# The channel MLP's second layer: 256 features per bank visit instead of 128

## The chip, the cores and the metric

The kernel runs on one core of a Trainium2 chip (trn2). The core has five engines that run side by side and wait for each other by semaphores: TensorE (PE in the profile; its weight loads are listed apart as PEld), VectorE (DVE), ScalarE (ACT), GpSimd (POOL) and SyncE (SP), which issues most of the DMAs from one queue, in order. The metric is the device time of one execution in microseconds (us); lower is better.

## The reference

Attention with a threshold, per batch row (8 of them) and head (8), over 576 tokens of 64 features, and then an MLP mixer on the row of 576 tokens by 512 features:

```python
scores = scale * np.matmul(q, k.transpose(0, 1, 3, 2))
thresh = np.max(scores, axis=-1, keepdims=True) - tau
scores = np.where(scores >= thresh, scores, -1000000000.0)
...
attn = attn / (np.sum(attn, axis=-1, keepdims=True) + 1e-09)
out = np.matmul(attn, v)
# heads side by side: x is (8, 576, 512)
h = np.maximum(x.transpose(0, 2, 1) @ w_tok1, 0.0) @ w_tok2
u = x + h.transpose(0, 2, 1)
h2 = np.maximum(u @ w_ch1, 0.0) @ w_ch2
return u + h2
```

`w_tok1` is 576 x 256, `w_tok2` 256 x 576, `w_ch1` 512 x 1536 and `w_ch2` 1536 x 512. All is float32. The last two lines are the channel MLP; its second layer is the product with `w_ch2`.

## The kernel before

The program is emitted by a planner (`Scheduler`). Each piece of work is an operation with an engine, an estimated cost, a rank and the operations it depends on. The planner keeps a clock for each engine, picks whatever can start first (at equal times the lower rank), and calls the function that emits its instructions. The order so found is each engine's program order on the chip; the estimates are used for nothing else.

Attention runs in 72 rounds, 9 to a batch row. A round is: scores on TensorE (S, L825), row maxima on VectorE (`mx`, L842), a bias on GpSimd (`bias`, L848), masks on ScalarE (L858), exponentials on ScalarE (L868), a scaling on GpSimd (L285), a blockwise transpose on VectorE (`T`, L315) and its completion by DMA (`eT<-T`, L327). Three units of such probabilities make one product with the values (V, L365 and L370). While attention of row b runs, the MLPs of the row before fill TensorE between the rounds: the token MLP (turns L435, first layer L454, second layer L472, added into `xT` by L483) and then, for a group of 256 tokens, the channel MLP. A round of rows 1 to 7 is held back until enough of that filling has been done (`self.done` against a plan), as long as there is other work for TensorE.

The channel MLP of a group is, for rows 1 to 6 (one group each; row 0 has two, which are done in another way, and what is put off is done after attention, by other code, from 903 us on):

- `turn_u` (L933, VectorE) transposes the group blockwise into the tile `us`, and `move_u` (SyncE, L940) completes it into `ut`. `us` is one buffer: it can be written only when the stores of the group before have read it.
- `ch1` (L948), 12 outputs of 4 products, each followed by a ReLU into `g` on ScalarE (L953) or VectorE (L956).
- `ch2` (L964), for each of 2 blocks of 128 tokens 4 outputs of 128 features, each the sum of 12 products; `leave` (L978, VectorE) adds the residual from `ut` and writes into `us`.
- `store` (L988, SyncE), one per block of tokens, when the block's outputs are in `us`.

Outputs of TensorE go to PSUM banks. While attention runs, two banks serve everything but the scores: values, token MLP and channel MLP. `banked` makes a pair of operations, the products, which take a free bank, and the eviction, which frees it; the products of an output are one piece and can't be interrupted. On VectorE, ScalarE and SyncE, too, an instruction that waits holds up all that is behind it in the order.

The spill of `xT` (L531) and the moves into `x_sb` (L406, L412) are other DMAs in SyncE's order. On the page, float32 products have two records each, so that an output of `ch2` shows as 24 records of L964.

Of the kernel before, what the change touches and what calls it, by code (L numbers as in the profile page):

```python
# [17 lines left out]
P = 128  # L18
# [3 lines left out]
def kernel(  # L22
# [38 lines left out]
    NCC = DM // P  # L61
    NJ = DCH // P
# [7 lines left out]
    work = ctx.enter_context(tc.tile_pool(name="work", bufs=2))  # L70
# [74 lines left out]
    wc2 = const.tile([P, NJ, DM], F32, name="wc2")  # L145
# [233 lines left out]
    class Step:  # L379


        def __init__(self, kind, cost, on, cost_out, work, leave, other=None):
            self.kind, self.cost, self.on, self.cost_out, self.work, self.leave = kind, cost, on, cost_out, work, leave
            self.other = other
# [167 lines left out]
    class Op:  # L552

        def __init__(self, eng, cost, fn, deps, after, rank, lag, row, index):
            self.eng, self.cost, self.fn, self.rank, self.lag, self.row, self.index = eng, cost, fn, rank, lag, row, index
            self.end, self.bank, self.frees, self.later, self.open, self.other = None, None, None, [], 0, None
            self.dmas, self.landed, self.shared = None, None, False
            self.deps = [d for d in deps if d is not None]
            for d in self.deps + [d for d in after if d is not None]:
                if d.end is None:  # L560
                    d.later.append(self)
                    self.open += 1
# [5 lines left out]
    class Scheduler:  # L568
# [22 lines left out]
        def banked(self, cost, work, on, cost_out, leave, deps=(), rank=5, row=None, rank_out=0, other=None):  # L591
            x = self.op("pe", cost, work, deps, rank, row=row)
            y = self.op(on, cost_out, leave, (x,), rank_out, row=row, other=other)
            x.bank = True
            y.frees = x
            return x, y

        def sure(self, x):
            t = max([d.landed + SPARE if d.landed else d.end + d.lag + SLACK * (d.eng != x.eng) for d in x.deps] + [0.0])
            if x.bank:  # L600
                t = max(t, min(b.free for b in self.banks if b.free is not None) + SLACK)
            return t
# [59 lines left out]
        def run(self, until):  # L662
            while not until():
                best = None
                for e in self.clock:
                    c = self.pick(e)
                    if c and (best is None or c[0][0] < best[0][0]):
                        best = c + (e,)
                if best is None:
                    assert all(x.end is not None for x in self.ops), [(x.eng, x.rank, x.index, x.open) for x in self.ops if x.end is None][:20]  # L670
                    return
                _, t, x, eng = best
                if eng == "pe" and t < WARM_UNTIL:
                    self.keep_warm(t)
                self.ready[x.eng].remove(x)
                if x.other:
                    self.ready[x.other[0]].remove(x)
                    if eng != x.eng:
                        x.eng, x.cost, x.fn = x.other
                if x.dmas:  # L680
                    x.end = self.transfer(t, *x.dmas)
                    x.landed = self.in_flight[-1]
                else:
                    x.end = t + x.cost
                self.clock[x.eng] = x.end
                if x.eng == "pe":
                    self.last_rank = x.rank
                if x.bank:
                    b = min((b for b in self.banks if b.free is not None), key=lambda b: b.free)
                    b.free = None  # L690
                    x.bank = b, b.pool.tile([P, MAIN], F32, tag=b.tag, name=f"bank_{x.index}")
                    x.fn(x.bank[1])
                    if x.row is not None:
                        self.done += x.cost
                elif x.frees:
                    b, tile_ = x.frees.bank
                    x.fn(tile_)
                    b.free = x.end + 0.15
                else:
                    x.fn()  # L700
                for y in x.later:
                    y.open -= 1
                    if not y.open:
                        self.enter(y)

    sched = Scheduler()
# [3 lines left out]
    def key_op(*key):  # L710
        return keyed.get(key)
# [165 lines left out]
    fills = {}  # L877
# [41 lines left out]
    def make_groups(b, halves):  # L919
        uT = xTs[b]  # L920
        reads = []
        for i in range(NOW[b]):
            s = {}
            n, nt = GR, GR // P

            def new_us(s=s, i=i):
                s["us"] = work.tile([P, nt, 4, NCC * 32], F32, tag="us", bufs=1, name=f"us_{b}_{i}")
# [27 lines left out]
            def relu_v(bank, j, s=s):  # L955
                nc.vector.tensor_scalar(out=s["g"][:, j, 0:n], in0=bank[:, 0:n], scalar1=0.0, scalar2=None, op0=ALU.max)  # L956

            def ch2(bank, t, c, s=s, i=i):
                to = bank[:, 0:P]
                t0 = GR * i + P * t  # L960
                if not b:
                    nc.tensor.matmul(to, lhsT=uT[:, c, t0 : t0 + P], rhs=ident, is_transpose=True, start=True, stop=False, skip_group_check=True)
                for j in range(NJ):
                    nc.tensor.matmul(  # L964
                        to,
                        lhsT=s["g"][:, j, P * t : P * t + P],
                        rhs=wc2[:, j, P * c : P * c + P],
                        start=(j == 0 and b > 0),
                        stop=(j == NJ - 1),
                        skip_group_check=True,  # L970
                    )

            def leave(bank, t, c, s=s):
                if not b and "us" not in s:
                    new_us(s)
                o = s["us"][:, t].rearrange("q a x -> q (a x)")[:, P * c : P * c + P]
                if b:
                    nc.vector.tensor_add(  # L978
                        out=o.rearrange("q (k d) -> q k d", k=4),
                        in0=bank[:, 0:P].rearrange("q (k d) -> q k d", k=4),  # L980
                        in1=s["ut"][:, t][:, :, 32 * c : 32 * c + 32],
                    )
                else:
                    nc.scalar.copy(out=o, in_=bank[:, 0:P])
# [12 lines left out]
            for j in range(NJ):  # L997
                x, y = sched.banked(
                    1.79,
                    lambda bank, j=j, f=ch1: f(bank, j),  # L1000
                    "act",
                    0.29,
                    lambda bank, j=j, f=relu: f(bank, j),
                    have + state["ch2"] + [key_op("pool", 7 + j)],
                    2,
                    b,
# [5 lines left out]
            seconds, stores, adds = [], [], []  # L1012
            for t in range(nt):
                outs = []
                for c in range(NCC):
                    x, y = sched.banked(
                        2.7 if b else 2.8,
                        lambda bank, t=t, c=c, f=ch2: f(bank, t, c),
                        "dve" if b else "act",
                        0.21,  # L1020
                        lambda bank, t=t, c=c, f=leave: f(bank, t, c),
                        relus + moved + (converted if not b else []) + (state["stores"] if not b else []),
                        2,
                        b,
                        1 if b else 0,
                    )
                    outs.append(y)
                    seconds.append(x)
                    if not b:
                        reads.append(x)  # L1030
                    fills[b] = fills.get(b, 0.0) + x.cost
                adds += outs
                stores.append(sched.op("sp", 0.35, lambda t=t, f=store: f(t), outs, 2, dmas=(1, 150, 0.35)))
            state["ch2"], state["stores"], state["adds"] = seconds, stores, adds
# [453 lines left out]
```

## Time and profile before

| | us |
|---|---|
| three runs | 1269.9, 1270.09, 1276.9 |
| median | 1270.09 |
| the profiled execution | 1273.39 |
| its span, first to last instruction | 1271.4 |
| mean granted TensorE clock | 0.991 |

| stage of the profiled execution | us | TensorE busy |
|---|---|---|
| 0 to 205: attention of rows 0 and part of 1, weights converted | 205.0 | 188.8 |
| 205 to 903: attention and the MLPs of the row before | 698.0 | |
| 903 to 1271.4: the token groups that were put off | 368.4 | 363.2 |

The profile is one execution on the chip. A row of the groups gives the line and engine, the operation, out<-in by the program's names with their shapes, the count, then busy time in us and mean duration in ns, and then the idle time of the engine just before these instructions with what ended it. A row of the timeline gives start and duration in us first; a row of the waits gives who waited for whom, then us in total, times, and the longest. Records of TensorE overlap: the time that a product takes in a run of them is read from start to start, not from its duration.

### The profile page before, as it was taken

The page shows a single profiled execution, that of the slowest core. Times are in us where ns is not written, and L with a number is a line of the kernel's source. Part 1 is how long each engine was busy: PE and PEld are TensorE (multiplying, and loading weights), DVE is VectorE, ACT ScalarE, POOL GpSimd, SP SyncE. Part 2 cuts the span into 40 slices and gives each one's busy share as a digit, 9 for nine tenths or more (in the row PEclk, how much of TensorE's full clock was granted, in tenths as well). Part 3 has the DMA queues.
Part 4 walks back from the last instruction along what each step waited for, and adds up shares of the span by engine and source line. Part 5 has one row for each costly group of instructions (what it writes and reads, how often), then busy time and mean ns, then how long its engine had stood idle before and what let it go on. Part 6 is the DMA issues. An engine that isn't in the chain of part 4 may idle for free.

```text
span 1271.4 us, 21773 instructions
## 1 busy us (share of the span) xinstructions
PE 1237.8 (97%) x8150; PEld 1015.3 (80%) x8150; DVE 755.0 (59%) x1163; ACT 564.0 (44%) x1233; POOL 315.4 (25%) x518
## 2 busy tenths in 40 slices
PE   8888999999999999999989999999999999999998
PEld 7656778797678778878867777888988888888887
DVE  6699982656666667756666756761443534444443
ACT  6998862554645545556465455531110202011120
POOL 4565641232223333323323322410001010000100
PEclk9899999999999999999999999999999999999999
DMA  9546985366777786786776875750212101021011
GB/s 167 139 124 166 214 212 131 87 128 160 168 164 175 160 169 150 165 178 137 179 148 135 187 159 111 179 150 1 60 23 67 34 25 42 18 67 25 26 34 33
DMA packets 324216, 149.23 MB, mean 117 GB/s; under 512 B 223696, under 2 KB 316880, under 8 KB 324112
## 3 DMA queue, kind: packets, MB, share of 16 engines
q1 hardware_dynamic: 322240, 147.64, 50.5%
q8 instruction: 64, 1.05, 0.4%
q10 hardware_dynamic: 1872, 0.21, 0.1%
q14 instruction: 40, 0.33, 0.1%
HBM read 47.32 MB, written 13.50 MB: 48 GB/s over the span
## 4 chain that ended last, share of the span: by engine, by line
PE 78%; SPq 6%; DVE 5%; DMA 5%; ACT 4%; issue 2%; POOL 0%; DVEq 0%; ACTq 0%; POOLq 0%
PE bank L964 11%; PE bank L948 10%; PE o L1309 10%; PE sc L825 9%; PE bank L370 7%; PE hx L1309 6%; PE bank L454 5%; PE hmm L1309 4%; PE oz L1309 4%; PE hz L1309 4%; PE bank L472 4%; SPq L327 3%; PE bank L365 2%; DVE mx L842 2%; ACT e L858 2%
## 5 line engine op out<-in xcount | busy, mean ns | idle before, releaser
L285 POOL TENSOR_SCALAR e<-e,rr 128x576 f32<-128x576 f32 x288 | 213.2, 758 | 299.1 <-DVE rr L277 286.6
L858 ACT ACTIVATE e<-sc,bias 128x576 f32<-128x576 f32 x288 | 194.1, 740 | 156.8 <-POOL bias L848 155.1
L842 DVE TENSOR_REDUCE mx<-sc 128x2 f32<-128x1152 f32 x144 | 188.1, 1347 | 58.9 <-PE sc L825 58.4
L868 ACT ACTIVATE e<-e,ntau 128x576 f32<-128x576 f32 x288 | 220.4, 778 | 0.3
L315 DVE STREAM_TRANSPOSE T<-e 128x1152 f32<-128x1152 f32 x126 | 170.0, 1362 | 36.1 <-POOL e L285 22.2
L948 PE MATMUL bank<-xT,wc 128*128 128x256 f32 x768 | 181.0, 389 | 6.1 <-ACT g L953 5.1
L964 PEld LDWEIGHTS bank<-wc,g 128*128 128x128 f32 x1536 | 178.0, 192 | 10.4 <-issue 2.4
L964 PE MATMUL bank<-wc,g 128*128 128x128 f32 x1536 | 181.4, 276 | 0.9 <-DVE xT L483 0.4
L948 PEld LDWEIGHTS bank<-xT,wc 128*128 128x128 f32 x768 | 144.2, 192 | 36.6 <-ACT g L953 6.5
L825 PE MATMUL sc<-kT,qT 64*128 64x192 f32 (+1 forms) x1920 | 168.8, 337 | 2.7 <-ACT e L858 2.7
L825 PEld LDWEIGHTS sc<-kT,qT 64*128 64x128 f32 (+1 forms) x1920 | 140.8, 179 | 32.1 <-issue 16.3
L370 PE MATMUL bank<-eT,lv 128*64 128x384 f32 (+1 forms) x1024 | 135.2, 406 | 0.0
L1392 POOL TENSOR_TENSOR us<-us,ut 128x256 f32<-128x256 f32 x27 | 22.4, 843 | 391.8 <-DVE us L1230 391.8
L370 PEld LDWEIGHTS bank<-eT,lv 128*64 128x64 f32 x1024 | 74.4, 137 | 49.7 <-issue 41.3
L848 POOL TENSOR_SCALAR bias<-mx,toff 128x2 f32<-128x2 f32 x144 | 38.8, 270 | 197.9 <-DVE mx L842 193.3
L454 PE MATMUL bank<-x_sb,w 128*128 128x256 f32 x320 | 72.8, 383 | 0.3 <-DVE eT L305 0.2
L472 PE MATMUL bank<-w,a 128*128 128x192 f32 (+1 forms) x256 | 72.8, 418 | 0.2 <-DVE xT L483 0.2
L454 PEld LDWEIGHTS bank<-x_sb,w 128*128 128x128 f32 x320 | 59.8, 190 | 11.3 <-issue 1.3
L953 ACT ACTIVATE g<-bank 128x256 f32<-128x256 f32 x66 | 25.3, 383 | 92.9 <-PE bank L948 92.7
L1357 ACT ACTIVATE ga<-hmm 128x256 f32<-128x256 f32 x30 | 11.5, 384 | 116.8 <-PE hmm L1309 116.8
L1230 DVE TENSOR_TENSOR temps<-hx,temps 128x256 f32<-128x256 f32 x60 | 25.1, 418 | 56.7 <-PE hx L1309 56.6
L868 ACT ACTIVATION_READ_ACCUMULATOR e<-e,ntau 128x1 f32 x288 | 58.4, 203 | 0.0
(133 smaller groups left out, 1519.6 us busy)
## 6 DMA issues: line engine op xcount, KB each, us to landing
eT<-T SPq DMA_DIRECT2D x504, 144.0 KB, 3.0
lk<-in_k_dram SPq DMA_DIRECT2D x126, 72.0 KB, 2.9
lq<-in_q_dram SPq DMA_DIRECT2D x124, 72.0 KB, 3.1
out_dram<-us SPq DMA_DIRECT2D x32, 256.0 KB, 2.1
ut<-us SPq DMA_DIRECT2D x128, 64.0 KB, 2.1
lv<-in_v_dram SPq DMA_DIRECT2D x112, 72.0 KB, 2.6
spare<-in_moe_w_ch_dram SPq DMA_DIRECT2D x8, 512.0 KB, 3.9
extra<-in_moe_w_ch_dram SPq DMA_DIRECT2D x8, 512.0 KB, 3.8
```

The source lines that it names most:

```text
L285: nc.gpsimd.tensor_scalar(out=eh, in0=eh, scalar1=rr[:, h : h + 1], scalar2=1.0, op0=ALU.mult, op1=ALU.mult)
L315: nc.vector.transpose(out=T.rearrange("p a (c x) -> p c a x", c=NK), in_=e.rearrange("p (c a x) -> p c a x", c=NK, a=4))
L370: nc.tensor.matmul(to[r], lhsT=lv[:, j, :], rhs=e[j], start=False, stop=(c == NI - 1), skip_group_check=True)
L454: nc.tensor.matmul(to, lhsT=w1[:, t, P * m : P * m + P], rhs=x(t), start=(t == 0), stop=(t == NT - 1), skip_group_check=len(products) > 1,)
L472: nc.tensor.matmul(bank[:, n * i : n * i + n], lhsT=hidden[b][:, m, P * c : P * c + P], rhs=w2[:, m, lo : lo + n], start=(m == 0), stop=(m ...
L825: nc.tensor.matmul(sc[h][rows, f, HT * k : HT * k + HT], lhsT=qT[r, cols], rhs=kT[r, HT * f : HT * f + HT], start=True, stop=True, skip_gr ...
L842: nc.vector.tensor_reduce(out=mx[:, h], in_=sc[h][:, :, 0 : 2 * HT].rearrange("p f (k x) -> p k f x", k=2), axis=AX.XY, op=ALU.max)
L858: nc.scalar.activation(out=eh, in_=part[h], func=AF.Prelu, bias=bias[:, h], scale=SCALE, alpha=STEEP)
L868: nc.scalar.activation(out=eh, in_=eh, func=AF.Exp, bias=ntau, accum_out=rs[:, h, 0:1])
L948: nc.tensor.matmul(bank[:, 0:n], lhsT=wc1[:, j, c, :], rhs=uT[:, c, GR * i : GR * i + n], start=(c == 0), stop=(c == NCC - 1))
L964: nc.tensor.matmul(to, lhsT=s["g"][:, j, P * t : P * t + P], rhs=wc2[:, j, P * c : P * c + P], start=(j == 0 and b > 0), stop=(j == NJ - 1 ...
L1309: nc.tensor.matmul(ps, lhsT=l, rhs=r, start=start and x == 0, stop=x == len(pairs) - 1, skip_group_check=not start)
```

## The change

In rows 1 to 6 an output of the second layer has 256 columns (two of the four blocks of features), made in two parts of six products; other work can come between the parts, while the bank stays taken. The second part ranks just ahead of other work of its rank. A group's 8 outputs of 128 columns become 4 of 256, its 8 evictions become 4 of twice the width, and its two stores stay. The planner's estimates become 2.6 for a part (2.7 for an output before) and 0.35 for an eviction (0.21 before), and the second part counts into `self.done` as well. Row 0 stays as it was.

```diff
+        def banked_in_two(self, cost, work, on, cost_out, leave, deps, rank, row, rank_out):
+            x = self.op("pe", cost, lambda bank: work(bank, 0), deps, rank, row=row)
+            z = self.op("pe", cost, lambda: work(x.bank[1], 1), (x,), rank - 0.1)
+            z.counts = True
+            y = self.op(on, cost_out, leave, (z,), rank_out, row=row)
+            x.bank = True
+            y.frees = x
+            return z, y
...
                     x.fn()
+                    if x.counts:
+                        self.done += x.cost
...
-            def ch2(bank, t, c, s=s, i=i):
-                to = bank[:, 0:P]
+            wide = 2 if b else 1
+
+            def ch2(bank, t, c, half=None, s=s, i=i, wide=wide):
+                to = bank[:, 0 : wide * P]
...
-                for j in range(NJ):
+                for j in range(NJ) if half is None else range(NJ // 2 * half, NJ // 2 * half + NJ // 2):
                     nc.tensor.matmul(
                         to,
                         lhsT=s["g"][:, j, P * t : P * t + P],
-                        rhs=wc2[:, j, P * c : P * c + P],
+                        rhs=wc2[:, j, P * c : P * c + wide * P],
...
                     nc.vector.tensor_add(
-                        out=o.rearrange("q (k d) -> q k d", k=4),
-                        in0=bank[:, 0:P].rearrange("q (k d) -> q k d", k=4),
-                        in1=s["ut"][:, t][:, :, 32 * c : 32 * c + 32],
+                        out=o.rearrange("q (w k d) -> q w k d", w=wide, k=4),
+                        in0=bank[:, 0 : wide * P].rearrange("q (w k d) -> q w k d", w=wide, k=4),
+                        in1=s["ut"][:, t].rearrange("q k (c d) -> q c k d", c=NCC)[:, c : c + wide],
                     )
...
-                for c in range(NCC):
-                    x, y = sched.banked(
-                        2.7 if b else 2.8,
-                        lambda bank, t=t, c=c, f=ch2: f(bank, t, c),
+                for c in range(0, NCC, wide):
+                    make = sched.banked_in_two if b else sched.banked
+                    x, y = make(
+                        2.6 if b else 2.8,
+                        lambda bank, *half, t=t, c=c, f=ch2: f(bank, t, c, *half),
                         "dve" if b else "act",
-                        0.21,
+                        0.35 if b else 0.21,
```

More of the change, by code (lines that the diff above doesn't have):

```diff
@@ L556, in __init__ @@
             self.end, self.bank, self.frees, self.later, self.open, self.other = None, None, None, [], 0, None
-            self.dmas, self.landed, self.shared = None, None, False
+            self.dmas, self.landed, self.shared, self.counts = None, None, False, False
             self.deps = [d for d in deps if d is not None]
@@ L971, in ch2, with leave @@
                     )
-            def leave(bank, t, c, s=s):
+            def leave(bank, t, c, s=s, wide=wide):
                 if not b and "us" not in s:
                     new_us(s)
-                o = s["us"][:, t].rearrange("q a x -> q (a x)")[:, P * c : P * c + P]
+                o = s["us"][:, t].rearrange("q a x -> q (a x)")[:, P * c : P * c + wide * P]
                 if b:
                     nc.vector.tensor_add(
-                        out=o.rearrange("q (k d) -> q k d", k=4),
-                        in0=bank[:, 0:P].rearrange("q (k d) -> q k d", k=4),
-                        in1=s["ut"][:, t][:, :, 32 * c : 32 * c + 32],
+                        out=o.rearrange("q (w k d) -> q w k d", w=wide, k=4),
+                        in0=bank[:, 0 : wide * P].rearrange("q (w k d) -> q w k d", w=wide, k=4),
+                        in1=s["ut"][:, t].rearrange("q k (c d) -> q c k d", c=NCC)[:, c : c + wide],
                     )
@@ L1030, in make_groups @@
                         reads.append(x)
-                    fills[b] = fills.get(b, 0.0) + x.cost
+                    fills[b] = fills.get(b, 0.0) + x.cost * wide
                 adds += outs
```

## The prediction

> **What bounds the kernel now.** The first view is the page's busy times with its forty slices.
>
> ```profile
> PE 1237.8 (97%) x8150; PEld 1015.3 (80%) x8150; DVE 755.0 (59%) x1163; ACT 564.0 (44%) x1233; POOL 315.4 (25%) x518
> PE   8888999999999999999989999999999999999998
> PEclk9899999999999999999999999999999999999999
> ```
>
> TensorE is busy for 1237.8 of 1271.4 us, in every slice after the fourth at 90% or more, while no other engine passes 60%. A second taken from TensorE's own work, or from the time it stands idle, is therefore a second of the kernel; a second taken from VectorE is worth something only where TensorE was waiting for VectorE.
>
> The next view is what TensorE waited for between 205 and 903 us, the stretch that holds all the work the change touches (us in total, times, longest).
>
> ```profile
> PE bank L948 <- ACT g L953: 5.1, 3, 2.6
> PE bank L365 <- DMA x_sb<-extra: 1.9, 1, 1.9
> PE bank L962 <- DVE rr L276: 1.2, 1, 1.2
> PE bank L365 <- DVE xT L483: 1.0, 1, 1.0
> PE bank L365 <- DMA lv<-in_v_dram: 1.0, 2, 0.6
> ...
> PE bank L964 <- ACT g L953: 0.4, 1, 0.4
> PE bank L964 <- ACT x_sb L439: 0.2, 1, 0.2
> ```
>
> The second layer is L964 and its eviction L978. No row says that TensorE waited for L978: the 48 evictions that become 24 are hidden already, so their saving goes on no path. What TensorE did wait for most is L953, the eviction of the *first* layer, 5.1 us in three waits. I come back to it, since the change reorders the work around it.
>
> **The products.** The change leaves the arithmetic alone: per row, 8 outputs of 12 products with 128 columns become 4 outputs of 12 products with 256 columns. The profile shows two records for each product. The timeline of TensorE (start, duration, then the instruction) shows 24 narrow records, which are one output before, and two stretches of the late part of the kernel with 12 records of the wide shape, which is exactly one part of an output after.
>
> ```profile
> 876.51 2.84 PE L964 MATMUL bank<-wc,g 128*128 128x128 f32 x24
> 879.19 1.46 PE L472 MATMUL bank<-w,a 128*128 128x384 f32 x4
> ...
> 963.35 2.75 PE L1309 MATMUL oz<-w2s,x_sb 128*128 128x256 f32 x12
> 965.94 2.75 PE L1309 MATMUL o<-w2s,x_sb 128*128 128x256 f32 x12
> ```
>
> From start to start the narrow stretch takes 879.19 - 876.51 = 2.68 us, 111.7 ns a record; the wide one 965.94 - 963.35 = 2.59 us, 215.8 ns a record. Both multiply the same number of columns, so a part saves 0.09 us. There are 6 rows x 4 outputs x 2 parts = 48 parts: **-4.3 us**, all on the path. It lies between 0 (if wide records in this place are as slow per column as narrow ones; slower than that no row of the wide shape is, so a loss is left out) and about 5 (the four times are rounded to 0.01, which allows 0.104 a part). I take 4.3, because these rows have the very shape, 128x256, from the same weights.
>
> The Trainium skill has its own price for this: "TensorE: Matmul & The Clock Gate", in the section on 56 and 53.3 ns, says that back-to-back matmuls cost a fixed 2.5 ns or so beside their columns. As an estimate, 576 records fewer (1152 narrow become 576 wide) at 2.5 ns would be 1.4 us instead of 4.3; the two rows differ from it, at 2 x 111.7 - 215.8 = 7.6 ns for each pair of narrow records, and the rows decide.
>
> A stretch of the second layer also costs something where it borders on attention work, which uses half of the array's rows or columns. The next two pairs of rows show the same kind of work (eight records of L472) between two neighbours of attention, and between two of the second layer.
>
> ```profile
> 502.80 1.57 PE L472 MATMUL bank<-w,a 128*128 128x192 f32 x8
> 504.29 1.90 PE L825 MATMUL sc<-kT,qT 64*128 64x192 f32 x20
> ...
> 887.13 1.47 PE L472 MATMUL bank<-w,a 128*128 128x192 f32 x8
> 888.43 2.84 PE L964 MATMUL bank<-wc,g 128*128 128x128 f32 x24
> ```
>
> Start to start 1.49 against 1.30 us: 0.19 us for going into such work and out again. Counted in the orders in which the two kernels issue their products, TensorE changes between full-array work, scores and values 218 times before and 220 times after. That is one more stretch, **+0.2 us**. The two parts of an output are often apart (21 of 24 times), but an output has two parts where there were two outputs, so the number of pieces that can be slotted between rounds is the same.
>
> **The evictions.** The group rows of VectorE price them.
>
> ```profile
> L978 DVE TENSOR_TENSOR us<-bank,ut 128x128 f32<-128x128 f32 x48 | 13.2, 275 | 34.6 <-PE bank L964 34.5
> L1230 DVE TENSOR_TENSOR us<-o,ut 128x256 f32<-128x256 f32 x10 | 4.2, 425 | 12.9 <-PE o L1309 12.9
> ```
>
> 48 at 275 ns become 24 of the L1230 shape at 425 ns: 13.2 us become 10.2. VectorE gets 3 us back and TensorE nothing, **0**, because no wait on L978 stands in the table above. What covers the longer eviction is the product behind it on the other bank, at least 1.30 us from start to start by the L472 rows above; without that cover it would cost its extra 0.15 us, 24 times, 3.6 us.
>
> **The order.** Costs in the planner fall from 2.7 an output to 2.6 a part, 21.6 to 20.8 a row, and with them what is counted as done; attention rounds that are held until enough is done come later relative to the second layer, and bank turns move. From row 1's second layer on (about 355 us) the whole order of all engines is new. So the question is which of the waits of before were accidents of the old order. The two longest are one accident, twice. Here it is at 638 us: SyncE's queue, VectorE, ScalarE and TensorE in turn (in brackets the idle time and its releaser), and then the second instance on TensorE.
>
> ```profile
> 621.75 0.66 SPq L531 DMA_DIRECT2D spill<-xT  x1
> 622.50 6.47 SPq L327 DMA_DIRECT2D eT<-T  x8
> 629.08 2.48 SPq L412 DMA_DIRECT2D x_sb<-extra  x4
> 631.60 0.59 SPq L988 DMA_DIRECT2D out_dram<-us  x1
> ...
> 620.44 0.25 DVE L978 TENSOR_TENSOR us<-bank,ut 128x128 f32<-128x128 f32 x1
> ...
> 634.41 2.08 DVE L933 STREAM_TRANSPOSE us<-xT 128x512 f32<-128x512 f32 x2 [3.95 <-DMA out_dram<-us]
> 636.42 1.33 DVE L315 STREAM_TRANSPOSE T<-e 128x1152 f32<-128x1152 f32 x1
> 637.68 2.58 DVE L842 TENSOR_REDUCE mx<-sc 128x2 f32<-128x1152 f32 x2
> ...
> 639.39 1.37 ACT L858 ACTIVATE e<-sc,bias 128x576 f32<-128x576 f32 x2 [3.94 <-POOL bias L848]
> 640.65 0.39 ACT L953 ACTIVATE g<-bank 128x256 f32<-128x256 f32 x1
> ...
> 641.09 3.55 PE L948 MATMUL bank<-xT,wc 128*128 128x256 f32 x8 [2.60 <-ACT g L953]
> ...
> 739.69 2.09 DVE L933 STREAM_TRANSPOSE us<-xT 128x512 f32<-128x512 f32 x2 [3.95 <-DMA out_dram<-us]
> ...
> 746.38 3.54 PE L948 MATMUL bank<-xT,wc 128*128 128x256 f32 x8 [2.08 <-ACT g L953]
> ```
>
> Read from the top: the last eviction of row 3's group is done at 620.7, but its store is issued at 631.60, because the spill, eight eT moves and four x_sb moves stand ahead of it in SyncE's queue. The next group's turn (L933) overwrites `us` and waits 3.95 us for that store. Behind it VectorE has the maxima (L842), behind these ScalarE the masks (L858), and behind the masks, in ScalarE's own order, the eviction (L953) for whose bank TensorE waits 2.60 us. TensorE then still pays: the windows below are the stretches after the two waits.
>
> ```profile
> 640.80:644.20 3.40, 3.11 (x7) 2.52 (x8) 1.49 (x2) 3.40 (x8) 0.00 (x0) 0.51 0.70 179
> 746.70:750.10 3.40, 3.40 (x10) 2.28 (x10) 1.18 (x3) 3.40 (x9) 0.00 (x0) 0.50 0.85 191
> ```
>
> The seventh figure is the granted clock: half speed for 3.40 us. At half speed 1.7 us of work is lost, so the two waits cost 2.60 + 2.08 + 2 x 1.7 = 8.1 us, 4.3 and 3.8 each. The skill's page on TensorE, in its section on the clock gate, ties the drop to a whole idle window of about 3.4 us; here idle stretches of 2.60 and 2.08 us were followed by it, so the trace's shorter ones are what I reckon with.
>
> In the order that the changed kernel issues, the last stores of rows 3 and 4 stand *ahead* of the spill, the eight eT moves and the x_sb moves on SyncE. They no longer sit behind 0.66 + 6.47 + 2.48 = 9.6 us of issuing, which is more than the 3.95 us that the turn waited. What is late next there is the turn's own place on VectorE, which then waits for nothing. I take both waits as gone: **-8.1 us** (between 0, if other transfers hold the stores up as long, and -8.1).
>
> The new order has two places of its own with the same shape. Row 2's last store now comes behind the spill, eight eT moves and the x_sb moves, and row 3's turn stands directly ahead of the maxima on VectorE. And before row 5's second layer the last first-layer eviction stands on ScalarE behind three masks of a round issued just before. Each could cost nothing or, by the two instances above, up to 4.3 us; I count one of the two at nearly full price, **+4.0 us**. Whoever waits for them is again the next product that needs the bank.
>
> **Sum.** -4.3 + 0.2 + 0 - 8.1 + 4.0 = -8.2 us. The profiled execution took 1273.39 us (span 1271.4 and 2.0 around it), 3.3 above the median of 1270.09; the terms are differences within its span, so it would come to 1265.2, and the median to 1270.1 - 8.2 = **1261.9 us**.
>
> **Rivals.** *The waits only change places.* The waits of before were made by queues that drift from the planner's times, and the new order drifts as much: the 8.1 us come back elsewhere. Then only the products count, 1270.1 - 4.1 = 1266. For it: the rows quoted of TensorE's waits have releasers on three engines and on the DMA queue. Against: the two large ones have one cause, which the new order removes. Chance 0.25.
>
> *Both large waits go and no new one comes.* -4.1 - 8.1 = -12.2, and up to another 3 from the small rows of the first table: 1255 to 1258. For it: half of what I fear in the two new places is a guess. Against: both places have the exact shape that cost 4 us. Chance 0.18, two thirds of it below 1257.4.
>
> *Slower, by a held bank.* Until attention ends there are two banks for all of this. An output now keeps its bank across both parts, and in 21 of 24 cases other work comes between; in three of these there are two banked pieces between, which must share the one bank left, and after each second part the next piece wants a bank that VectorE has just been asked to free. Where such an eviction is queued behind masks or maxima, TensorE waits as at 638 us, at 4.3 us with the clock. With the two old waits gone and -12.2 as the starting point, three such waits give 1270.1 + 0.7 and four 1275; the point from which it decides is the third. For it: 5.1 us of such waits on L948 now, with each bank turned once per output. Against: in 18 of 21 cases there is one banked piece between, and a part of 2.59 us is cover enough for evictions of 0.28 to 0.43 us. Chance 0.12.
>
> *The change does not do what it says.* If wide records pace like two narrow ones, nothing is left of the 4.3, and with my other terms it is -3.9, 1266; the rows at 963.35 speak against it. Chance 0.03.
>
> **How the numbers follow.** My forecast has 0.42. About 1% (12.7 us) is what a measurement of this kernel can tell from no change, so the bounds are 1257.4 and 1282.8. The forecast with its unknowns runs from 1257 (one new wait absent) to 1267 (both there at full price). For eight in ten I add most of the faster rival and the slower one up to four waits: 1255 to 1274. Faster by over 1%: 0.12 from the second rival and 0.04 from the forecast's edge, 0.16. Slower by over 1% needs six waits of 4.3 us in the third rival, 0.04. Within 1%: 0.80.
>
> **What would show it.** In the profile after: L964's line with 1152 fewer 128-column records and 576 of 256 columns, twelve of them 2.59 us from start to start; 24 evictions near 425 ns; the store of rows 3 and 4 issued before the spill, no wait of L933 on `out_dram` followed by a wait of the first layer on L953; the granted clock without half-speed stretches after 64 us or with one. It would be wrong if half-speed stretches turn up at other places, if the waits of TensorE between 205 and 903 us stay at the 10.8 us that the quoted rows add up to, or if a wait on the second layer's eviction appears in the table.

## The result, and the profile after

The changed kernel took 1265.64 us in the median of 6 runs (1264.42 to 1266.97), the kernel before 1271.89 in 6 runs beside it (1269.9 to 1276.9): 6.2 us less. The ratio of the means is 0.9947, with a 95% interval of 0.9927 to 0.9967, so 6.7 us or 0.5% faster, between 4.2 and 9.3 (gains over the kernel before go by such ratios from here on). The forecast was -8.2 us and 1261.9, the range 1255 to 1274. On another chip, with 9 and 20 runs, the ratio was 0.9962 (0.9947 to 0.9977), 4.8 us.

In the changed kernel's line numbers L964 of before is L977, L978 is L991, L948 is L959, L953 is L964, L933 is L944 and L988 is L1001. The page after, in the lines shown of before:

```profile
PE 1231.5 (97%) x7574; PEld 991.7 (78%) x7574; DVE 751.0 (59%) x1136; ACT 566.2 (45%) x1236; POOL 315.7 (25%) x518
PE   8898999999899999999999999999999999999998
PEclk9899999999999999999999999999999999999999
```

576 records fewer, 6.3 us of TensorE less (part of it half clock, which is taken off further below), and still 97%: what was taken away was TensorE's own. The groups of the second layer and its eviction and two neighbouring parts in the timeline show the new shape:

```profile
L977 PE MATMUL bank<-wc,g 128*128 128x256 f32 x576 | 133.0, 381 | 3.4 <-ACT g L964 3.0 <-ACT x_sb L439 0.2 <-DVE us L991 0.2
L991 DVE TENSOR_TENSOR us<-bank,ut 128x256 f32<-128x256 f32 x24 | 10.0, 416 | 36.0 <-PE bank L977 33.9 <-DMA lq<-in_q_dram 1.9
```

```profile
886.90 2.75 PE L977 MATMUL bank<-wc,g 128*128 128x256 f32 x12
889.49 1.46 PE L472 MATMUL bank<-w,a 128*128 128x192 f32 x8
```

A part of twelve records takes 889.49 - 886.90 = 2.59 us, as forecast, and an eviction 416 ns (425 forecast). What TensorE waits for between 205 and 903 us, the same view as before:

```profile
PE bank L365 <- DMA x_sb<-extra: 3.2, 1, 3.2
PE bank L977 <- ACT g L964: 3.0, 2, 2.7
PE bank L959 <- ACT xT L374: 1.9, 1, 1.9
PE bank L365 <- issue: 1.3, 1, 1.3
PE bank L365 <- DMA lv<-in_v_dram: 1.0, 1, 1.0
...
PE bank L977 <- DVE us L991: 0.2, 1, 0.2
```

The two waits of the first layer on L953 are gone. Two others have come, on L374 (the eviction of a value product) and on L964 (the first layer's eviction, now for the second layer's first product). The last row is a wait on the wide eviction, 0.2 us in all. All rows of this view add up to 12.0 us; those of the kernel before add up to 12.8 (the 10.8 of the prediction are the rows that it quotes), so the waits were hardly less.

The stores of rows 3 and 4 stand where the prediction saw them, ahead of the spill and the eT moves (SyncE's queue and, last, VectorE's turn, which waits for nothing):

```profile
622.18 0.57 SPq L1001 DMA_DIRECT2D out_dram<-us  x1
622.85 1.12 SPq L531 DMA_DIRECT2D spill<-xT  x1
624.06 6.47 SPq L327 DMA_DIRECT2D eT<-T  x8
...
724.49 1.65 SPq L1001 DMA_DIRECT2D out_dram<-us  x2
726.24 0.57 SPq L531 DMA_DIRECT2D spill<-xT  x1
...
628.92 2.09 DVE L944 STREAM_TRANSPOSE us<-xT 128x512 f32<-128x512 f32 x2
```

And the two new places are there too. First row 3's turn, from SyncE to TensorE; then the eviction behind masks before row 5's second layer:

```profile
523.66 2.50 SPq L327 DMA_DIRECT2D eT<-T  x4
526.20 0.61 SPq L1001 DMA_DIRECT2D out_dram<-us  x1
...
530.18 2.14 DVE L944 STREAM_TRANSPOSE us<-xT 128x512 f32<-128x512 f32 x2 [4.72 <-DMA out_dram<-us]
532.23 2.59 DVE L853 TENSOR_REDUCE mx<-sc 128x2 f32<-128x1152 f32 x2
...
533.95 2.64 ACT L869 ACTIVATE e<-sc,bias 128x576 f32<-128x576 f32 x4 [2.92 <-POOL bias L859]
...
537.24 0.53 ACT L374 COPY xT<-bank 128x192 f32<-128x192 f32 x2
...
537.82 0.48 PE L959 MATMUL bank<-xT,wc 128*128 128x256 f32 x1 [1.88 <-ACT xT L374]
...
763.64 2.00 ACT L869 ACTIVATE e<-sc,bias 128x576 f32<-128x576 f32 x3 [2.01 <-POOL bias L859]
765.54 0.38 ACT L964 ACTIVATE g<-bank 128x256 f32<-128x256 f32 x1
...
765.97 2.21 PE L977 MATMUL bank<-wc,g 128*128 128x256 f32 x9 [2.71 <-ACT g L964]
```

The first reads like the instance at 638 us of before: the store behind other issues, the turn 4.72 us behind the store, the maxima behind the turn, the masks behind the maxima, and behind them in ScalarE's order an eviction that TensorE needs. The second has no store in it: the eviction stands behind three masks, which waited 2.01 us for their bias.

### The profile page after: what moved, and what is told of

It reads as the page before. It is cut to its first block, busy times and chain, and to the rows that moved or that the text cites. A ratio compares the mean times of both kernels' runs of the same rounds, so it can differ in the third digit from the quotient of the medians.

```text
span 1265.2 us, 20604 instructions
## 1 busy us (share of the span) xinstructions
PE 1231.5 (97%) x7574; PEld 991.7 (78%) x7574; DVE 751.0 (59%) x1136; ACT 566.2 (45%) x1236; POOL 315.7 (25%) x518
## 4 chain that ended last, share of the span: by engine, by line
PE 80%; SPq 6%; DVE 6%; DMA 4%; ACT 2%; issue 2%; POOL 0%; DVEq 0%; ACTq 0%; POOLq 0%
PE bank L977 11%; PE bank L959 10%; PE o L1323 10%; PE sc L836 10%; PE bank L370 7%; PE hx L1323 6%; PE bank L454 5%; PE bank L472 4%; PE hz L1323 4%; PE oz L1323 4%; PE hmm L1323 4%; SPq L327 3%; PE bank L365 2%; DVE mx L853 2%; SPq L106 2%
## 5 line engine op out<-in xcount | busy, mean ns | idle before, releaser
L977 PE MATMUL bank<-wc,g 128*128 128x256 f32 (+1 forms) x960 | 179.8, 341 | 3.4 <-ACT g L964 3.0
L959 PE MATMUL bank<-xT,wc 128*128 128x256 f32 x768 | 177.4, 384 | 2.2 <-ACT xT L374 1.9
L977 PEld LDWEIGHTS bank<-wc,g 128*128 128x128 f32 x960 | 153.8, 193 | 27.3 <-issue 5.1
L959 PEld LDWEIGHTS bank<-xT,wc 128*128 128x128 f32 x768 | 142.7, 190 | 31.3 <-issue 7.7
L964 ACT ACTIVATE g<-bank 128x256 f32<-128x256 f32 x72 | 27.6, 383 | 98.1 <-PE bank L959 97.8
```

What stands on the lines that cost most here:

```text
L959: nc.tensor.matmul(bank[:, 0:n], lhsT=wc1[:, j, c, :], rhs=uT[:, c, GR * i : GR * i + n], start=(c == 0), stop=(c == NCC - 1))
L977: nc.tensor.matmul(to, lhsT=s["g"][:, j, P * t : P * t + P], rhs=wc2[:, j, P * c : P * c + wide * P], start=(j == 0 and b > 0), stop=(j == ...
```

## The experiments

**The width by itself.** The changed kernel with its order, parts, evictions and bank visits, but with narrow products:

```diff
+                    for w in range(wide):
                         nc.tensor.matmul(
-                            to,
+                            to[:, P * w : P * w + P],
...
-                            rhs=wc2[:, j, P * c : P * c + wide * P],
-                            start=(j == 0 and b > 0),
+                            rhs=wc2[:, j, P * (c + w) : P * (c + w) + P],
+                            start=(j == 0 and w == 0 and b > 0),
```

> The changed kernel with its order, its two parts, its 24 evictions and its bank visits kept, but each product of 256 columns made as two of 128 into the two halves of the same bank. Theory (width pays by itself): 48 parts x 0.09 us come back, 4.3 us over the changed kernel, so 1.9 us under the kernel before by the medians (-6.2 + 4.3); a part takes 2.68 us from start to start instead of 2.59. Rival A (all of the gain is the new order): stays 6.2 us under the kernel before. Rival B (all of the gain is the width): comes back to the kernel before, 0 +- 1 us.

Measured: 1270.73 us, 0.9988 of before (0.9968 to 1.0008), so 1.5 us under it, where 1.9 was expected. The kernel before itself had medians of 1269.5 to 1271.9 on the chips used, so I ran the changed and the narrow kernel once more on one chip:

> The changed kernel again, beside the next kernel on one chip, since the medians of the kernel before differ by 2.4 us between the chips used so far. Theory (48 parts x 0.09 us of work, and waits that come out about even over many executions): 4 to 6 us under the kernel before, 0.9953 to 0.9969. Rival (the first ratio, with its 6.2 us, holds the new order's gain too): 0.9947 or below.

> The changed kernel with two products of 128 columns for each of 256, again, on the chip of the run above. Theory: 4 to 5 us slower than the changed kernel on this chip, within 2 us of the kernel before. Rival A (all of it is the order): as fast as the changed kernel within 1 us.

Measured on that chip: the changed kernel 1265.16 us, 0.9962 (0.9947 to 0.9977); the narrow one 1270.73, 0.9999 (0.9985 to 1.0013). The intervals don't meet. With narrow products all of the gain is gone: the change is worth its width, some 4.7 us, and its new order nothing that these runs can tell from zero. Rival A falls. A narrow part takes 897.08 - 894.40 = 2.68 us in the profile of the last of these runs, as expected:

```profile
894.40 2.84 PE L978 MATMUL bank<-wc,g 128*128 128x128 f32 x24
897.08 1.47 PE L472 MATMUL bank<-w,a 128*128 128x192 f32 x8
```

The profiles say the same without the waits. The next rows are windows from the first second-layer product of row 1 (up to there the two kernels are one program) to the first product of the late part; the second figure is the window's length, the third TensorE's busy time. They are of before in its first and a second profile, of the changed kernel in two, and of the narrow one.

```profile
359.79:903.67 543.88, 534.75 (x3963) 429.80 (x3961) 342.58 (x485) 269.12 (x585) 143.72 (x252) 0.99 0.65 147
```

```profile
361.77:899.64 537.87, 531.46 (x3963) 427.51 (x3961) 340.21 (x484) 269.07 (x585) 144.28 (x252) 1.00 0.65 148
```

```profile
363.18:897.27 534.09, 526.27 (x3388) 404.87 (x3387) 336.44 (x455) 271.40 (x588) 143.85 (x252) 1.00 0.66 149
```

```profile
360.26:896.64 536.38, 526.68 (x3388) 404.79 (x3387) 338.36 (x456) 271.49 (x588) 143.94 (x252) 1.00 0.66 149
```

```profile
364.81:905.04 540.23, 533.56 (x3964) 428.78 (x3962) 336.41 (x455) 271.24 (x588) 143.82 (x252) 0.99 0.65 147
```

The first has two half-speed stretches in it, which make 3.4 of its busy us, and the last has two as well; without them TensorE's work is 531.35 and 531.46 before, 526.27 and 526.68 after, and 530.2 with narrow products. So the change takes away 4.9 us of TensorE's work, 3.7 of them by the width; the other 1.2 come with the order and the halved number of bank visits, and which of the two wasn't tried apart. The idle time (length less busy) was 9.1 and 6.4 us before, 7.8 and 9.7 after, and 6.0 in a third profile of the changed kernel: these few do not show that it fell.

**The two waits of before.** The kernel before with a second buffer for `us`, every engine's order as it was:

```diff
...
-                s["us"] = work.tile([P, nt, 4, NCC * 32], F32, tag="us", bufs=1, name=f"us_{b}_{i}")
+                s["us"] = work.tile([P, nt, 4, NCC * 32], F32, tag="us", bufs=2, name=f"us_{b}_{i}")
...
```

> The kernel before with two buffers for us (the buffer's room comes from one weight-loading buffer that moves into it); the order on every engine is that of the kernel before. It takes away the wait of the turn (L933) for the last store of the group before, and nothing else. Theory (the two waits at 638 and 744 us come from that store and cost 2.60 + 2.08 us and twice 1.7 us of half clock): 8.1 us faster than before, about 0.994, no idle of L933 on out_dram, no half-speed stretch between 400 and 900 us. Rival (the maxima would be late anyway, by the transposes or the exponentials): 0 to 2 us faster, TensorE still waits 2 us at the two places.

Measured: 1267.44 us in 12 runs, 0.9979 (0.9959 to 0.9999), 2.7 us. Its waits of TensorE on the first layer's evictions:

```profile
PE bank L948 <- DVE g L956: 0.8, 3, 0.3
...
PE bank L948 <- ACT g L953: 0.4, 1, 0.4
```

The mechanism holds: with the store out of the way the 5.1 us on L953 are 0.4, and no half-speed stretch falls between 400 and 900 us. The size doesn't: 2.7 us and not 8.1. So the kernel before was profiled once more.

> The kernel before once more, for a second profile of it. In the first profile the part that both kernels have in common (up to the first second-layer product of row 1) took 359.8 us, 1.5 to 3.7 less than in the five other profiles, and the part behind it 543.9. Theory now (the two waits of the turn are there in every execution, but half clock follows a TensorE wait of about 2 us only sometimes): both waits are seen again, of 1.5 to 2.7 us, fewer than two half-speed stretches between 400 and 900 us, and the middle part takes about 539 us. Rival (first profile typical): 544 with two half-speed stretches.

It took 1269.2 us. VectorE's two turns, and TensorE's two waits, in the second profile:

```profile
634.70 2.09 DVE L933 STREAM_TRANSPOSE us<-xT 128x512 f32<-128x512 f32 x2 [3.10 <-DMA out_dram<-us]
...
737.28 2.11 DVE L933 STREAM_TRANSPOSE us<-xT 128x512 f32<-128x512 f32 x2 [2.71 <-DMA out_dram<-us]
...
641.39 1.99 PE L948 MATMUL bank<-xT,wc 128*128 128x256 f32 x8 [1.78 <-ACT g L953]
...
743.98 1.99 PE L948 MATMUL bank<-xT,wc 128*128 128x256 f32 x8 [0.86 <-ACT g L953]
```

The same places, 1.78 + 0.86 = 2.6 us instead of 4.7, and the clock stayed up after both: eight records take 1.92 us here (643.31 - 641.39 to the next instruction, by the same timeline), not 3.5. The middle window is 537.9 us, near the 539 expected. The first profile had drawn the long side of both: the window of the run with two buffers, 535.85 us, is 8.0 us shorter than that of the first profile and 2.0 shorter than that of the second.

**The waits of the changed kernel.**

> The changed kernel once more, for a second profile. Theory: the three waits of the first profile (row 3's first layer at about 536, values at 547, the second layer behind masks at 763) are there again, each 1 to 3 us; the middle part takes 534 us, plus 1.7 for each half-speed stretch in it, of which 0 to 2 are expected. Rival (they were accidents of one execution): other places.

It took 1266.35 us, with waits of 2.07, 1.43 and 1.85 us at 537, 548 and 765 us: the same three places. Its middle window is 536.4 us, more than the 534 expected, for a fourth wait: the values at 753 us waited 2.15 us, where it had been 0.97. In a third profile, the changed kernel's run on the other chip, the first and the last were 2.40 and 1.86 us, with one half-speed stretch at 536.5.

> The changed kernel with two buffers for us, its order kept. The changed kernel's profile has one such wait left that reaches TensorE (row 3's turn waits 4.7 us for a store, then the maxima, and TensorE waits 1.9 us at 536 us) and one of 0.8 us in front of row 6's turn. Theory: 1.9 us faster than the changed kernel, up to 3.6 in executions where the clock drops after it; 8 to 10 us under the kernel before. Rival (the wait only moves): the same as the changed kernel within 1 us.

Measured: 1264.18 us, 0.9941 (0.9924 to 0.9958). That is 7.5 us under the kernel before, where 8 to 10 was expected, against 6.7 and 4.8 for the changed kernel with one buffer. The wait at 536 us is gone from its profile, but the value product at 548 us waits 2.80 us there, where the two profiles above have 1.34 and 1.43, and the intervals overlap: a gain over the changed kernel is not shown, and the rival that the wait only moves is not out.

**Without the split.**

```diff
-                    make = sched.banked_in_two if b else sched.banked
+                    make = sched.banked
...
-                        2.6 if b else 2.8,
+                        5.2 if b else 2.8,
...
-                    fills[b] = fills.get(b, 0.0) + x.cost * wide
+                    fills[b] = fills.get(b, 0.0) + x.cost
```

> 256 columns per output, but the twelve products in one piece that nothing can interrupt (planner's cost 5.2, one count), so the order differs from both kernels. Theory (the width pays 4.3 us wherever it is, the split only sets where other work can come in): between 4.3 us under the kernel before and 4 us over the changed kernel, so -4 +- 4 us against before. Rival (without the split attention comes late behind pieces of 5.2 us): slower than the changed kernel by over 6 us, more waits of TensorE on values and on the eviction of the first layer.

Measured: 1271.65 us, 1.0006 (0.9989 to 1.0023), 0.8 us over the kernel before and so outside what I expected, though the interval reaches into it. TensorE's work is the least of all, but it waits:

```profile
362.37:899.92 537.55, 525.62 (x3388) 405.37 (x3387) 340.10 (x451) 273.08 (x594) 143.84 (x252) 1.00 0.66 150
```

```profile
PE bank L959 <- DVE g L967: 5.9, 3, 3.0
...
PE bank L472 <- DVE xT L483: 2.4, 2, 2.0
```

537.55 - 525.62 = 11.9 us idle in the window, with the longest waits now behind evictions on VectorE. One order can't tell whether pieces of 5.2 us do this by themselves or by accident; the changed kernel, with the split and the order that comes with it, is 5.6 and 7.5 us ahead of this one by its two ratios, on different chips.

**A new order, and nothing else.** The kernel before with the planner's 2.7 for an output made 2.6:

> The kernel before with one figure changed: the planner's cost of a narrow second-layer output is 2.6 instead of 2.7. No instruction differs but the order, which is new from row 1 on. It tells how much a new order alone is worth by accident. Theory (an order's worth is set by which stores and masks happen to stand in front of what TensorE needs): any value within 5 us of before, 0.996 to 1.004, with the waits at other places than before. Rival (the order of before was as good as any other): slower by more than 5 us.

Measured: 1268.95 us, 0.9983 (0.9962 to 1.0004): 2.2 us, within the 5 expected and not told apart from before. TensorE's waits had other places (values at 479 and 751 us, the second layer at 454 and 493), and none of the two of before. TensorE's work in the middle window is 531.81 us, no less than before: a new order need not bring the 1.2 us that came with the changed kernel's, which points to the bank visits without showing it.

**SyncE's issues.** All profiles so far show a value product at about 340 us that waits 1.9 to 4.1 us while SyncE issues without a break. First attempt, half of the q and k loads from ScalarE's queue:

```diff
-                        lambda lo=lo: load_qk(n, (nc.sync,) * 2, range(lo, lo + 2)),
+                        lambda lo=lo: load_qk(n, (nc.sync, nc.scalar), range(lo, lo + 2)),
```

> The changed kernel with two buffers for us, and with the loads of k issued from ScalarE's queue instead of SyncE's (about 0.5 us each, 4 for each of 31 pairs). SyncE issues without a break before the value product of row 2 at 338 us, which waited 1.9 to 4.1 us in all six profiles. Theory (SyncE's queue is what makes these transfers late): the wait at 338 us shrinks by 1 us or more and the value products later on wait less; 2 to 5 us faster than with two us buffers alone, so 1259 to 1262. Rival (ScalarE's issues delay masks and evictions as much as they help): no faster than 1264, with more waits of TensorE for ScalarE.

Measured: 1271.59 us, 1.0002 (0.9985 to 1.0018), where 1259 to 1262 was expected. The theory's edit was a bad one: the wait is still there with 3.29 us (at 348 us), and in the first 205 us, where ScalarE also empties the banks of row 0's transposes, TensorE now waits 10.1 us for that in 12 waits; the changed kernel's first profile has 4.6 in 9:

```profile
PE bank L300 <- ACT eT L305: 10.1, 12, 3.4
```

Second attempt: the work stays where it is, and the planner is told what SyncE's issues cost.

```diff
-                    dmas=(4, 147, 0.645),
+                    dmas=(4, 147, 0.72),
...
-                        dmas=(2, 107, 0.58),
+                        dmas=(2, 107, 0.62),
...
-        moved = [sched.op("sp", 1.2, lambda i=i: move_main(i), turns + before, 0, dmas=(1, 131, 0.645)) for i in range(4)]
+        moved = [sched.op("sp", 1.2, lambda i=i: move_main(i), turns + before, 0, dmas=(1, 131, 0.7)) for i in range(4)]
```

> The changed kernel with two buffers for us, and with the planner told what SyncE's issues cost in the profiles: 0.72 us for each of a move's four (0.645 before), 0.62 for the loads of q and k (0.58), 0.70 for the moves into x_sb (0.645). The instructions are the same, their order is new. Theory (the long waits come from SyncE running behind the plan): less idle time of TensorE between 205 us and the late part than the 13 to 15 us of the changed kernel, by 2 to 5 us, and 2 to 5 us faster than it. Rival (one new order is as good as another): the same as the changed kernel within 2 us, idle time of 12 to 16 us at other places.

> The changed kernel with the three issue costs of SyncE as measured (0.72, 0.62, 0.70), but with the one buffer for us that it had. The order on the four engines looked at is that of the run before, so it tells which of its two edits brought the time. Theory (the plan's issue costs made the waits, and a true plan also puts the turn where its store has landed): 1257.5 to 1260, at most 2 us slower than with two buffers. Rival (the second buffer did much of it): 1262 or more, with TensorE waits behind turns that wait for a store.

Measured: 1257.45 us with the second buffer, 0.9900 of before (0.9883 to 0.9916), and 1257.42 us without it, 0.9900 (0.9879 to 0.9921). Beside the changed kernel on the same chip (1265.16) the first is 7.7 us faster, more than the 2 to 5 expected: three figures of the plan brought more than the change itself, and the second buffer then adds nothing. Both runs have one and the same order, so they are one new order, and how much of it is owed to truer figures and how much to accident is not shown. The new figures are means, too: in the changed kernel's first profile the eT moves follow one another at 0.73 us in the mean and 0.65 in the median, which is the old figure; in the rows above four took 2.50 us and eight took 6.47. TensorE's waits between 205 and 903 us, without the second buffer:

```profile
PE bank L365 <- DMA x_sb<-extra: 2.9, 1, 2.9
PE bank L365 <- DVE xT L483: 1.3, 2, 0.9
PE bank L959 <- DVE g L967: 1.1, 3, 0.5
PE bank L472 <- DVE xT L483: 0.4, 1, 0.4
PE bank L435 <- ACT x_sb L439: 0.2, 1, 0.2
```

5.9 us in all, against 12.0 in the changed kernel's first profile. The wait at 340 us remains, and with it some 3 us that no run here explained.

## Why the prediction was right, and where it was not

**The products (-4.3 us): right.** 2.59 us a part, as read off the late stage, and 3.7 us of TensorE's work by the width, 4.7 us by the two ratios on one chip. The prediction's upper bound was a little low: four times rounded to 0.01 us allow 0.11 us a part, 5.3 us and not 5. The estimate of 1.4 us from the fixed 2.5 ns a record of the Trainium skill ("TensorE: Matmul & The Clock Gate", the section on 56 and 53.3 ns) is further from the measured 3.7 than the 4.3 of the rows.

**The changes of the array's use (+0.2 us): too small to see.** With the new order and narrow products TensorE's work was 1.2 us less than before, not 0.2 more.

**The evictions (0): right.** 24 at 416 ns. The one wait on them is 0.2 us.

**The two old waits (-8.1 us): the step that failed.** The cause was right, store behind issues, turn behind store, eviction behind masks: the order took the waits away, and so did the second buffer. But I priced them from one execution, with 2.60 and 2.08 us of idle and half clock after both. A second profile has 1.78 and 0.86 and no half clock, and twelve runs without them gain 2.7 us (0.1 to 5.2). The term should have been near 2.7. In the forty slices the prediction also passes over an 8 behind the fourth: slice 21, 636 to 668 us, where the first of the two waits falls.

**The two new waits (+4.0 us): right in place, in size by luck.** I had named two and counted one, with its half clock. Both came, at 1.88 + 2.71, 2.07 + 1.85 and 2.40 + 1.86 us in three profiles, 4.6, 3.9 and 4.3, and only one of the six was followed by half clock. One wait at the full price and two at half of it come to about the same.

With -2.7 in the place of -8.1, and 4.9 us of TensorE's work in all, the sum is -4.9 - 2.7 + 4.3 = -3.3 us; measured were -6.7 (-9.3 to -4.2) and -4.8 (-6.7 to -2.9), and the second interval holds it. What is left, 1.5 to 3.4 us, was not taken apart; the smaller waits, which the order re-made as well, are in it. The forecast of -8.2 lies inside the first interval and outside the second. That the time came out inside the range says little for the sum: the kernel before, at 1270.1, lies inside it as well.

**The signs of error.** Three of those that the prediction names turned up. The waits between 205 and 903 us stayed, at 12.0 against 12.8 us; a wait on the second layer's eviction is in the table; and half-speed stretches stand at other places, 205 and 342 us, both ahead of row 1's second layer, where the change does not reach. The first one is the telling one: the prediction expected 4 us less of waiting and half clock, and the narrow runs show no such gain.

**The rivals.** "The waits only change places" (-4.1) has the mechanism that was measured, and I had given it 0.25: with narrow products in the new order, at 0.9999, nothing is left of the gain. Its figure is also the nearer one on the second chip; on the first the forecast is. The held bank made no waits of the kind I feared; the changed kernel's waits are behind stores and masks, as before. The rival that the width does nothing is out.

## What to carry to other kernels

Look for the shape of an instruction elsewhere in the same trace before pricing it: the wide product's pace was there to read, and it held to the hundredth of a us. A wait read off one execution is a draw, not a price: profile the kernel before twice, and count a wait at what it costs on average. Where a planner decides the order, check its estimates against the spacing of the issues in the trace first: three issue costs of SyncE, raised by 7 to 12%, made an order that brought more than the change did, though one order can't tell how much of that was accident.

## What the runs showed of the hardware

Half clock after a TensorE wait depends on the wait's length and on where it falls. Over the 14 profiles, between 195 and 910 us, 40 waits of TensorE lasted over 1.7 us: of the 20 under 2.3 us, 5 were followed by half clock, of the 11 from 2.3 to 3 us 6, of the 9 above 3 us 7. Each such stretch lasted 3.4 us or twice that, and within a profile all of them start on one grid of 3.41 us: in the changed kernel's first profile the two at 205.33 and 341.87 us are 40 such steps apart. Where the grid lies differs between executions.

Divided into the windows of its grid, a profile shows what decides: how long TensorE stands idle inside one window. In 20 windows of the 14 profiles that was 1.99 us or more, and 18 of them were followed by half clock (the other two had 2.00 us); of the windows at full clock with less idle time none was. The rows below are two windows each, where the third figure is TensorE's busy time and the 1.00 or 0.50 near the end the clock. In the changed kernel's first profile the wait of 2.71 us at 766 us lies across two windows, with 3.41 - 1.54 = 1.87 and 3.41 - 2.56 = 0.85 us idle, and the clock stays up:

```profile
761.71:765.12 3.41, 1.54 (x9) 1.04 (x7) 2.80 (x3) 1.48 (x3) 0.53 (x2) 1.00 0.69 140
765.12:768.53 3.41, 2.56 (x12) 2.20 (x12) 2.01 (x5) 3.41 (x8) 0.00 (x0) 1.00 0.78 174
```

In its third profile the shorter wait of 2.40 us at 536 us lies in one window, with 3.41 - 1.01 = 2.40 us idle, and half clock follows:

```profile
533.05:536.46 3.41, 1.01 (x5) 0.77 (x5) 1.82 (x2) 3.41 (x10) 2.90 (x4) 1.00 0.47 99
536.46:539.87 3.41, 3.41 (x14) 2.50 (x14) 1.28 (x3) 2.02 (x6) 1.17 (x2) 0.50 0.51 107
```

So a wait of 2 to 3 us at one place can cost half clock in one execution and not in the next, as the two old waits did.

The Trainium skill's page "TensorE: Matmul & The Clock Gate", in its part on the clock gate, ties the drop to an idle window of about 3.4 us whose phase is its own. The grid here agrees with that, but the window need not be idle throughout: of the 35 waits here that were shorter than 3.4 us, 13 were followed by the drop.

The stretch up to row 1's second layer, which the change doesn't touch, took between 359.8 and 364.8 us in eleven profiles of kernels that share its order; in them the wait at 340 us lasted 1.9 to 4.1 us. That is as much as the whole change brought.
